# Attention and two MoE layers: weight stores of the first seven-product layer on ScalarE's queue, and its conversion steps apart

## The chip, the cores and the metric

The kernel runs on one core of a Trainium2 chip. The metric is the time of one execution on the device, in microseconds (us), as the median of several runs. In the profile, PE is TensorE (PEld its weight loads), DVE is VectorE, ACT is ScalarE, POOL is GpSimd and SP is SyncE, which here begins DMAs; SPq is SP's queue of them. L1206 is line 1206 of the kernel before.

## The reference

```python
# q, k, v: 8 batches x 8 heads x 576 tokens x 64
q_s = softmax(q, axis=-1);  k_s = softmax(k, axis=2)
attn = q_s @ (k_s^T @ v)                       # per batch and head
x = attn as 4608 tokens x 512
g = x @ w_gate                                 # 512 x 1536
x = (g * sigmoid(g) * (x @ w_val)) @ w_out     # 1536 x 512
h = x @ w_in                                   # 512 x 2048
out = where(h > 0, h, exp(min(h, 0)) - 1) @ w_out2   # 2048 x 512
```

The weights come as 64-bit floats, seen as pairs of 32-bit words.

## The kernel before

**Stages.** Tokens go in nine blocks of 512. `run_a` takes the blocks i = 0 to 8 in turn (to about 580 us): for each it works on the first half of the first MoE's features, six chunks f of 128, each in three substeps s: the gate product (`proj`), the value product, and the product with w_out of the chunk before (`emit_B`, L792 to L794). Beside this it prepares the attention of the blocks ahead: the tables `PLAN0`, `PLAN1` and `PLAN` say in which (f, s) a step such as `kv`, `turn1` or `kturn` is called, by `side_1a`. From about 580 to 1020 us the other half of the features runs with seven products in place of eight (`unit_b`, `step_b`, `single_b`, `step_s`; `product`, L1082): two blocks are cut in quarters, and the products M1 to M7 take sums of quarters of the input and of the weights. From 1020 us on the second MoE (`run_2`, `step`) does the same with its own weights.

**Splitting.** A product has 32-bit operands as a high part in a shorter format (ACT copies) and the rest (a subtraction on DVE or POOL). `part_split` (L1052 on ACT, L1053 on DVE) does this for a weight read back from DRAM; `splits` collects such jobs, `splits_due` and `run_splits` call them.

**Conversion.** `conv` is called beside the products and makes 32-bit weights of the chunks: `conv_load` (raw, SP), `conv_scale` (cg, ACT L189), `conv_bits` (DVE L204, L207, L211 into one of four buffers cd), `conv_split`. For a pair of chunks of the later half `sums_out` builds the sums of quarters on POOL (L252 to L255, st) and stores seven pieces (L265, sfg, sfv, sd); wo and wp chunks are stored by L236 (wb, wd). `defer(n, fn)` calls fn n substeps later, through `aged`.

**Attention round trips.** q is turned by way of DRAM: `qturn` (DVE, qn), `qout` (L534, dq), `qin` (L542, qT), then PE's `xT` (L622). `kturn` makes the maximum of k, stores it (L398, dk) and reads it back spread over the partitions (L400, mb). `load_q` (L353, L363) and `load_v` (L338) fetch the next block's inputs.

**Operands of the seven products.** `xd_tick` goes through six columns: it reads four quarters back (`xd_rows`, yr, L991), makes differences on POOL (`xd_open`, L1001), the high part on ACT (L1044), the low part on POOL (L1017, `xd_lo`), and stores both (L1019, xd). `x_small` and `x_big` load them for the second MoE; `load_s` and `load_p` load its weights (s<-sd, w<-wd).

Each engine takes its instructions in program order; SP is one queue, and a DMA that waits there holds all behind it.

## Time and profile before

| | |
|---|---|
| median of three runs | 1779.06 us (1778.4 to 1781.88) |
| profiled execution, its own time | 1786.1 us |
| its span | 1784.3 us |
| mean granted clock of PE | 0.974 |
| busy: PE, DVE, ACT, POOL | 1686.5, 1165.0, 799.9, 288.7 us |
| DMA | 351.95 MB, 197 GB/s over the span |

A row of waits says which instruction waited, which one released it, and for how long. A timeline row has the start, the duration, engine and line, out<-in, and the number of like instructions that were merged; the brackets give the idle time of the engine before it. In a table by stage, PEclk is the granted share of TensorE's full clock (1.00 is 2.4 GHz, 0.50 is 1.2).

### The profile page before, as it was taken

How to read it: one execution, taken by the hardware profiler on the slowest of the kernel's cores; microseconds unless marked ns; L12 is line 12 of the kernel's file. 1: busy time of each engine (PE TensorE's matmuls, PEld its weight loads, DVE VectorE, ACT ScalarE, POOL GpSimd, SP SyncE). 2: the span in 40 equal slices, each digit the busy share in tenths (PEclk: the TensorE clock that was granted, in tenths of full speed). 3: DMA queues.
4: the chain of work that ended last, by engine and by line, in shares of the span. 5: the costliest groups of instructions: out<-in, count | busy, mean ns of one | idle time of the engine just before them, and what ended most of it. 6: DMA issues, size and time to landing. Idle time of an engine off the chain costs nothing.

```text
span 1784.3 us, 22221 instructions
## 1 busy us (share of the span) xinstructions
PE 1686.5 (95%) x8228; PEld 1376.4 (77%) x8228; DVE 1165.0 (65%) x1758; ACT 799.9 (45%) x1339; POOL 288.7 (16%) x238
## 2 busy tenths in 40 slices
PE   5899898888999899998989889999999999999999
PEld 4677686666777688886878768888888888888887
DVE  7857796768667765664655476757674877466574
ACT  4635244334324442322422365646564755355353
POOL 3611132223015202353341100000000000000000
PEclk9999998998999999999999899999999999999999
DMA  9465877884667666878595945272612543352511
GB/s 279 123 166 164 245 212 226 220 257 150 220 204 284 222 235 225 291 253 313 198 355 210 395 138 222 96 271 69 250 74 100 182 189 125 135 188 72 212 48 71
DMA packets 192459, 351.95 MB, mean 197 GB/s; under 512 B 50144, under 2 KB 131040, under 8 KB 178400
## 3 DMA queue, kind: packets, MB, share of 16 engines
q1 hardware_dynamic: 192352, 350.55, 58.2%
q8 instruction: 64, 1.05, 0.2%
q14 instruction: 43, 0.35, 0.1%
HBM read 234.36 MB, written 116.14 MB: 196 GB/s over the span
## 4 chain that ended last, share of the span: by engine, by line
PE 75%; DMA 8%; DVE 7%; ACT 4%; issue 2%; POOL 2%; SPq 1%; DVEq 0%; POOLq 0%; ACTq 0%
PE p L1082 27%; PE y L794 11%; PE y L792 11%; PE y L793 11%; PE a L811 5%; PE a L812 5%; PE a L815 4%; DMA sd<-cd 1%; DMA ys<-ev 1%; DMA ev<-yp 1%; PE t L622 1%; DMA s<-sd 1%; PE t L464 1%; DVE u L1206 1%; DMA q<-in_q 1%
## 5 line engine op out<-in xcount | busy, mean ns | idle before, releaser
L1206 DVE TENSOR_TENSOR u<-u,p 128x512 f32<-128x512 f32 x315 | 216.0, 686 | 237.4 <-PE p L1082 212.8
L1082 PE MATMUL p<-xp,s 128*128 128x512 f32 x1344 | 326.0, 396 | 29.3 <-DVE u L1206 26.9
L1082 PEld LDWEIGHTS p<-xp,s 128*128 128x128 f32 x1344 | 255.0, 191 | 88.1 <-DVE u L1206 32.5
L1082 PE MATMUL p<-xs,s 128*128 128x512 f32 (+1 forms) x1260 | 274.7, 372 | 2.8 <-ACT th L1438 2.8
L1082 PEld LDWEIGHTS p<-xs,s 128*128 128x128 f32 x1260 | 224.5, 192 | 45.2 <-ACT th L1438 3.6
L794 PE MATMUL y<-w,g 128*128 128x512 f32 x576 | 225.1, 391 | 0.6
L792 PE MATMUL y<-w,g 128*128 128x512 f32 x576 | 224.3, 389 | 0.8 <-ACT g L1121 0.8
L793 PE MATMUL y<-w,g 128*128 128x512 f32 x576 | 224.2, 389 | 0.0
L811 PE MATMUL a<-x,w 128*128 128x512 f32 x424 | 174.4, 411 | 4.0 <-DVE th L842 3.0
L812 PE MATMUL a<-x,w 128*128 128x512 f32 x424 | 170.5, 402 | 0.0
L1101 DVE SCALAR_TENSOR_TENSOR th<-e,th 128x512 f32<-128x512 f32 x144 | 99.3, 690 | 101.5 <-ACT e L1096 100.0
L1094 ACT ACTIVATE e<-u 128x512 f32<-128x512 f32 x108 | 67.7, 627 | 147.5 <-DVE u L1206 147.5
L794 PEld LDWEIGHTS y<-w,g 128*128 128x128 f32 x576 | 108.1, 188 | 26.4 <-DVE g L1130 4.2
L792 PEld LDWEIGHTS y<-w,g 128*128 128x128 f32 x576 | 108.2, 188 | 23.4 <-ACT g L1121 1.2
L793 PEld LDWEIGHTS y<-w,g 128*128 128x128 f32 x576 | 108.1, 188 | 22.2
L1121 ACT ACTIVATE g<-th 128x512 fp32r<-128x512 f32 (+1 forms) x160 | 91.3, 580 | 67.8 <-DVE th L1107 67.8
L1130 DVE TENSOR_TENSOR g<-th,g 128x512 fp32r<-128x512 f32 (+1 forms) x160 | 100.0, 634 | 32.0 <-ACT g L1121 29.6
L815 PE MATMUL a<-x,w 128*128 128x512 f32 x424 | 113.8, 390 | 0.6 <-POOL w L244 0.6
L811 PEld LDWEIGHTS a<-x,w 128*128 128x128 f32 x424 | 82.9, 196 | 30.0 <-issue 7.5
L824 ACT ACTIVATE g<-th 128x512 fp32r<-128x512 f32 x54 | 33.9, 629 | 150.9 <-DVE th L842 150.9
L812 PEld LDWEIGHTS a<-x,w 128*128 128x128 f32 x424 | 83.1, 196 | 16.8
L815 PEld LDWEIGHTS a<-x,w 128*128 128x128 f32 x424 | 80.2, 189 | 18.1 <-POOL w L244 1.0
(204 smaller groups left out, 2728.3 us busy)
## 6 DMA issues: line engine op xcount, KB each, us to landing
xp<-xd SPq DMA_DIRECT2D x32, 1024.0 KB, 10.3
xs<-xd SPq DMA_DIRECT2D x51, 512.0 KB, 7.3
xd<-xst SPq DMA_DIRECT2D x42, 512.0 KB, 7.7
raw<-in_moe_w_out SPq DMA_DIRECT2D x26, 512.0 KB, 5.0
s<-sbg SPq DMA_DIRECT2D x12, 1024.0 KB, 6.9
s<-sbv SPq DMA_DIRECT2D x12, 1024.0 KB, 7.4
yp<-ev SPq DMA_DIRECT2D x9, 1024.0 KB, 4.3
xs<-ev SPq DMA_DIRECT2D x18, 512.0 KB, 6.9
```

What stands on the lines that cost most here:

```text
L792: nc.tensor.matmul(out=ps, lhsT=wh, rhs=xh, start=first, stop=False)
L793: nc.tensor.matmul(out=ps, lhsT=wh, rhs=xl, start=False, stop=False)
L794: nc.tensor.matmul(out=ps, lhsT=wl, rhs=xh, start=False, stop=last)
L811: nc.tensor.matmul(out=ps, lhsT=wh, rhs=x[:, c, 0, :], start=(c == 0), stop=False)
L812: nc.tensor.matmul(out=ps, lhsT=wh, rhs=x[:, c, 1, :], start=False, stop=False)
L815: nc.tensor.matmul(out=ps, lhsT=wl, rhs=x[:, c, 0, :], start=False, stop=(c == KD - 1))
L1082: nc.tensor.matmul(out=out_, lhsT=w, rhs=x, start=first and (q, c, k) == (0, 0, 0), stop=(c, k) == (1, 2), skip_group_check=True,)
L1094: nc.scalar.activation(out=e, in_=h, func=ACTF.Relu, scale=-1.0)
L1101: nc.vector.scalar_tensor_tensor(out=t, in0=e, scalar=1.0, in1=t, op0=ALU.add, op1=ALU.mult)
L1121: nc.scalar.activation(out=gt[:, 0, at:at + n], in_=t[:, q * n:(q + 1) * n], func=ACTF.Copy)
L1130: nc.vector.tensor_tensor(gt[:, 1, at:at + n], t[:, q * n:(q + 1) * n], gt[:, 0, at:at + n].bitcast(FP32), op=ALU.subtract,)
L1206: nc.vector.tensor_tensor(o, a, b, op=ALU.add)
```

## The change

1. The column chunks of the later weights are taken as 256 x 256 squares in another order (`wsrc_quads`, two DMAs per chunk), so that two quarters lie side by side; `sums_out` then stores four pieces, not seven. These stores, those of wb and wd, and those of yp (L868, `emit_B`) are begun on ACT's queue: 87 DMAs, where ACT had none. `conv` loads ahead of its other steps in this phase.
2. `qout` and the store of dk are called one substep later; the read of mb has a step of its own (`kspread`), `qin` of the first half and `load_q` too, and the second `qin` stands at (4, 0), not (3, 2).
3. `xd_tick`: another order of M1 to M7, with each sum made one operand ahead; rows are read up to two columns ahead and rest five ticks; the low parts go to DVE.
4. `part_split`'s subtraction can be deferred, each split can be held for some rounds, and the four first ones (`side_last`) go one per substep. `x_small` loads M7 and M5 a step earlier.

The diff, cut to its core:

```diff
@@ -79,6 +79,10 @@
...
 
+    def wsrc_quads(w, f):
+        r, c = f % 2 * 256, f // 2 * 256
+        return w[r:r + 256, c:c + 256].rearrange("(c p) (e f) -> p e c f", p=128, e=2)
+
     chunks = []
@@ -93,11 +97,11 @@
...
             for f in fs_:
-                chunks.append(((kind, f), wsrc_cols(w, f), True))
+                chunks.append(((kind, f), wsrc_quads(w, f), 2))
         for f in fs_:
...
     for f in range(F2):
-        chunks.append((("i", f), wsrc_cols(w_in2, f), True))
+        chunks.append((("i", f), wsrc_quads(w_in2, f), 2))
     for f in range(F2):
@@ -171,7 +175,11 @@
...
             rslot[n], t = slot4(kinds, [128, 512], "raw", I64)
-        if cols:
+        if cols == 2:
+            o = t.rearrange("p (e c f) -> p e c f", e=2, c=2)
+            for e in range(2):
+                nc.sync.dma_start(out=o[:, e], in_=src[:, e])
+        elif cols:
             nc.sync.dma_start(out=t.rearrange("p (c f) -> p c f", c=4), in_=src)
@@ -233,7 +241,7 @@
...
             d = ds.pop(n).bitcast(FP32)
-            defer(1, lambda: nc.sync.dma_start(out=wd[f] if kind == "p" else wb[f], in_=d))
+            defer(1, lambda: nc.scalar.dma_start(out=wd[f] if kind == "p" else wb[f], in_=d))
             return
@@ -247,8 +255,8 @@
...
         st = cv_p.tile([128, 4, 256], FP32, tag="st", name="st", bufs=1)
-        a11, a12 = d1[:, 0:256], d1[:, 256:512]
-        a21, a22 = d2[:, 0:256], d2[:, 256:512]
+        a11, a21 = d1[:, 0:256], d1[:, 256:512]
+        a12, a22 = d2[:, 0:256], d2[:, 256:512]
         nc.gpsimd.tensor_tensor(st[:, 0], a21, a22, op=ALU.add)
@@ -257,23 +265,29 @@
...
         st = sums(d1, d2)
-        srcs = [d1[:, 0:256], d1[:, 256:512], d2[:, 256:512]] + [st[:, k] for k in range(4)]
+        flat = lambda t: t.rearrange("p a n -> p (a n)")
 
         def store():
-            for a, src in enumerate(srcs):
-                part, k = PART[a]
-                nc.sync.dma_start(out=dst[part][:, k], in_=src)
+            nc.scalar.dma_start(out=dst[0][:, 0], in_=d1[:, 0:256])
+            nc.scalar.dma_start(out=flat(dst[1][:, 0:2]), in_=d2)
+            nc.scalar.dma_start(out=flat(dst[0][:, 1:4]), in_=flat(st[:, 0:3]))
+            nc.scalar.dma_start(out=dst[1][:, 2], in_=st[:, 3])
 
...
         free[0] = stage["split"]
+        ahead = stage["load"] >= NA1
+        if ahead:
+            conv_load()
+            conv_load()
         conv_split(eng or nc.gpsimd)
...
         conv_scale(wait)
-        conv_load()
-        conv_load()
+        if not ahead:
+            conv_load()
+            conv_load()
 
@@ -395,7 +409,9 @@
...
         )
-        nc.sync.dma_start(out=dk[b], in_=mk)
+        defer(0, lambda: nc.sync.dma_start(out=dk[b], in_=mk))
+
+    def kspread(b):
         mb = at1.tile([128, H, D], FP32, tag="km", name="mb")
@@ -865,7 +881,7 @@
...
                 nc.scalar.activation(out=ev[:, c, :], in_=acc[ph, i][c], func=ACTF.Copy)
-            nc.sync.dma_start(out=yps[i], in_=ev)
+            nc.scalar.dma_start(out=yps[i], in_=ev)
 
@@ -1001,12 +1017,12 @@
...
             ("M1", b11, lambda: sub(t1, b12, b11)),
-            ("M5", t1, lambda: sub(t2, b22, t1)),
-            ("M2", b21, lambda: None),
+            ("M2", b21, lambda: sub(t2, b22, t1)),
+            ("M5", t1, lambda: sub(b12, b22, b12)),
             ("M6", t2, lambda: sub(b21, b21, t2)),
+            ("M3", b22, lambda: None),
+            ("M7", b12, lambda: None),
             ("M4", b21, lambda: None),
-            ("M3", b22, lambda: sub(b12, b22, b12)),
-            ("M7", b12, lambda: None),
         ]
@@ -1014,7 +1030,7 @@
...
             m, c = xd_st["cur"][0:2]
-            nc.gpsimd.tensor_tensor(d[:, 1, :], src, d[:, 0, :].bitcast(FP32), op=ALU.subtract)
+            nc.vector.tensor_tensor(d[:, 1, :], src, d[:, 0, :].bitcast(FP32), op=ALU.subtract)
             defer(1, lambda: (
@@ -1024,11 +1040,11 @@
...
             e[0] += 1
-        if n < min(6, 2 * ready, k + 1) and room(ANY) >= 6:
+        if n < min(6, 2 * ready, k + 2) and room(ANY) >= (4 if n == k else 8):
             xd_rows(n)
...
         if xd_st["cur"] is None:
-            if k not in xd_r or xd_r[k][0] < 3:
+            if k not in xd_r or xd_r[k][0] < 5:
                 return
@@ -1040,31 +1056,37 @@
...
         at, d = slot4(ANY, [128, 2, TB], "xst")
+        nc.scalar.activation(out=d[:, 0, :], in_=src, func=ACTF.Copy)
         pre()
-        nc.scalar.activation(out=d[:, 0, :], in_=src, func=ACTF.Copy)
         xd_st["lo"] = (op, src, at, d)
...
 
-    def part_split(hi, lo):
+    def part_split(hi, lo, age=0):
         nc.scalar.activation(out=hi, in_=lo.bitcast(FP32), func=ACTF.Copy)
-        nc.vector.tensor_tensor(lo, lo.bitcast(FP32), hi.bitcast(FP32), op=ALU.subtract)
+        defer(age, lambda: nc.vector.tensor_tensor(
+            lo, lo.bitcast(FP32), hi.bitcast(FP32), op=ALU.subtract
+        ))
 
     def splits_due():
-        split_now.extend(splits)
-        splits.clear()
+        for e in list(splits):
+            if e[0]:
+                e[0] -= 1
+            else:
+                splits.remove(e)
+                split_now.append(e[1])
 
     def run_splits():
-        for fn in split_now:
-            fn()
+        for n, fn in enumerate(split_now):
+            fn(min(n // 2, 1))
         split_now.clear()
 
-    def load_p(f, kinds=ANY):
+    def load_p(f, kinds=ANY, hold=0):
         tag, t = slot4(kinds, [128, 2, 512], "w2")
         nc.sync.dma_start(out=t[:, 1].bitcast(FP32), in_=wd[f])
-        splits.append(lambda: part_split(t[:, 0], t[:, 1]))
+        splits.append([hold, lambda age: part_split(t[:, 0], t[:, 1], age)])
         W["p", f] = t
@@ -1246,6 +1268,8 @@
...
                 elu_hi(k12, e12)
+            aged()
+            aged()
             ends = [m() for m in mid]
@@ -1272,6 +1296,8 @@
...
             elu_lo(k12, e12)
+        aged()
+        aged()
         w = cg()
@@ -1309,12 +1335,14 @@
...
 
-    def load_s(g):
+    def load_s(g, hold=0):
         SW[g] = [s_tile((g + 2) % NG2, part) for part in range(2)]
...
             nc.sync.dma_start(out=t[:, :, 1, :].bitcast(FP32), in_=sd[g][part])
-            splits.append(lambda t=t: part_split(t[:, :, 0, :], t[:, :, 1, :]))
+            splits.append([
+                hold, lambda age, t=t: part_split(t[:, :, 0, :], t[:, :, 1, :], age)
+            ])
 
@@ -1391,10 +1419,10 @@
...
             nc.sync.dma_start(out=t[:, :, 1, :].bitcast(FP32), in_=sf[key][part])
-            splits.append(lambda t=t, part=part: (
-                part_split(t[:, :, 0, :], t[:, :, 1, :]),
+            splits.append([0, lambda age, t=t, part=part: (
+                part_split(t[:, :, 0, :], t[:, :, 1, :], age),
                 defer(2, lambda: nc.sync.dma_start(out=sb[key][part], in_=t.bitcast(FP32))),
-            ))
+            )])
 
@@ -1681,6 +1709,8 @@
...
                 load_yp(u[0])
+            if g == 1:
+                x_small(nxt, X_MID[0:2], ANY)
             step_s(u, g, mid, lambda: (aged(), xd_st["k"] < 6 and xd_tick(3)), g == NG1 - 1)
@@ -1690,7 +1720,7 @@
...
                 load_s(1)
-                x_small(nxt, X_MID, ANY)
+                x_small(nxt, X_MID[2:], ANY)
         while xd_st["k"] < 6 or later:
@@ -1699,9 +1729,9 @@
...
         for f in range(4):
-            load_p(f)
+            load_p(f, hold=1 + f // 2)
         carry = [lambda f=f: b_D(u[0], f) for f in (F1 - 2, F1 - 1)]
-        carry.append(lambda: (load_s(2), load_s(3), None)[2])
+        carry.append(lambda: (load_s(2), load_s(3, 1), None)[2])
         return carry
@@ -1726,7 +1756,8 @@
...
             splits_due()
-            run_splits()
+        if split_now and (ff, s) >= (3, 2):
+            split_now.pop(0)(0)
         if (ff, s) == (2, 0):
@@ -1748,7 +1779,8 @@
...
         "norm1": (2, 1), "turn1": (2, 2), "load_v2": (2, 2), "kmax0": (3, 0), "kmax1": (3, 2),
-        "xT0": (3, 2), "xT1": (3, 2), "in1": (3, 2), "kturn": (4, 0), "xT2": (5, 0), "xT3": (5, 0),
+        "in0": (2, 1), "load_q": (3, 0), "in1": (4, 0), "kspread": (4, 2),
+        "xT0": (3, 2), "xT1": (3, 2), "kturn": (4, 0), "xT2": (5, 0), "xT3": (5, 0),
         "qmax0": (4, 2), "qmax1": (5, 2),
@@ -1763,7 +1795,8 @@
...
         "qT2": (4, 0), "qT3": (4, 1), "xT2": (4, 2), "xT3": (4, 2),
-        "kmax0": (4, 1), "kmax1": (4, 2), "kturn": (5, 0), "qmax0": (5, 1), "qmax1": (5, 2),
+        "kmax0": (4, 1), "kmax1": (4, 2), "kturn": (5, 0), "kspread": (5, 2),
+        "qmax0": (5, 1), "qmax1": (5, 2),
     }
@@ -1797,8 +1830,11 @@
...
             st["sum"] = lambda: (qsum(t, 0), qsum(t, 1))
-            st["turn0"] = lambda: (qturn(t, 0), qout(t, 0), qin(t, 0))
-            st["turn1"] = lambda: (qturn(t, 1), qout(t, 1), u < NB and load_q(u))
+            st["turn0"] = lambda: (qturn(t, 0), defer(0, lambda: qout(t, 0)))
+            st["turn1"] = lambda: (qturn(t, 1), defer(0, lambda: qout(t, 1)))
+            if u < NB and i > 1:
+                st["load_q"] = lambda: load_q(u)
+            st["in0"] = lambda: qin(t, 0)
             st["in1"] = lambda: qin(t, 1)
@@ -1809,6 +1845,7 @@
...
                 st["kturn"] = lambda: kturn(u)
+                st["kspread"] = lambda: kspread(u)
         if u < NB:
@@ -1894,8 +1931,8 @@
...
                 if n == 0 and k < 2:
-                    load_p(4 + 2 * k)
-                    load_p(5 + 2 * k)
+                    load_p(4 + 2 * k, hold=1)
+                    load_p(5 + 2 * k, hold=1)
                 step(u, q, carry if k == 0 else [lambda: dd(u[0], k - 1)])
...
                 if turn:

```

On SP, in block i = 2, around the second `qin` (qT<-dq). raw, q, vtile, qT are buffers; sfv, wb, dq, dk are in DRAM. Before:

```order
L265 DMA sfv_132<-st 128x256 x3
L265 DMA sfv_133<-st 128x256
L534 DMA dq_156<-qn 32x8x128 x4
L353 DMA q<-in_q 64x2x256 x4
L363 DMA q<-in_q 64x2x256 x4
L338 DMA vtile<-in_v 128x8x64 x4
L338 DMA vtile<-in_v 64x8x64
L175 DMA raw<-in_moe_w_val 128x4x128
L177 DMA raw<-in_moe_w_out 128x512
L236 DMA wb_150<-cd 128x512
L236 DMA wb_151<-cd 128x512
L542 DMA qT<-dq_156 128x512 x2
```

and now:

```order
L558 DMA qT<-dq_156 128x512 x2
L662 DMA xs_175<-ev 128x1024
L352 DMA vtile<-in_v 128x8x64 x4
L352 DMA vtile<-in_v 64x8x64
L181 DMA raw<-in_moe_w_val 128x2x128 x2
L550 DMA dq_156<-qn 32x8x128 x4
L367 DMA q<-in_q 64x2x256 x4
L377 DMA q<-in_q 64x2x256 x4
L181 DMA raw<-in_moe_w_val 128x2x128 x2
L185 DMA raw<-in_moe_w_out 128x512
L558 DMA qT<-dq_156 128x512 x2
L412 DMA dk_163<-mk 16x32
```

The v loads stand ahead of dq, the seven sfv stores and two wb stores are gone, and dk's store and read stand right behind qT.

On ACT, in the same block, from the rest of silu (th, g) to the conversion. Before:

```order
L824 ACTIVATE g<-th 128x512
L189 ACTIVATE cg<-raw 128x512
L838 ACT_TABLE_LOAD
L838 ACTIVATE th<-a 128x512
L824 ACTIVATE g<-th 128x512
L189 ACTIVATE cg<-raw 128x512
L838 ACTIVATE th<-a 128x512
L189 ACTIVATE cg<-raw 128x512
L824 ACTIVATE g<-th 128x512
L601 ACTIVATE x<-t 128x512
```

and now:

```order
L840 ACTIVATE g<-th 128x512
L197 ACTIVATE cg<-raw 128x512
L854 ACT_TABLE_LOAD
L854 ACTIVATE th<-a 128x512
L840 ACTIVATE g<-th 128x512
L271 DMA sfv_132<-cd 128x256
L272 DMA sfv_133<-cd 128x512
L273 DMA sfv_132<-st 128x768
L274 DMA sfv_133<-st 128x256
L197 ACTIVATE cg<-raw 128x512
L854 ACTIVATE th<-a 128x512
L197 ACTIVATE cg<-raw 128x512
```

Four stores stand between two silu steps, and a wb store behind each of two conversions.

On DVE, at the passage from the first MoE's last step (silu's th and g, `step_s`) to the second MoE's first sums (u). s is a weight of the second MoE. Before:

```order
L1206 TENSOR_TENSOR u<-u,p_8250 128x512
L1053 TENSOR_TENSOR s_8175<-s_8175 128x4x256
L1053 TENSOR_TENSOR s_8176<-s_8176 128x3x256
L1053 TENSOR_TENSOR s_8179<-s_8179 128x4x256
L1053 TENSOR_TENSOR s_8180<-s_8180 128x3x256
L1547 TENSOR_TENSOR th<-th,u 128x256
L1547 TENSOR_TENSOR th<-th,p_8195 128x256
L1206 TENSOR_TENSOR u<-u,p_8250 128x512
L1206 TENSOR_TENSOR u<-u,p_8232 128x512
L1547 TENSOR_TENSOR th<-th,u 128x256 x2
L1553 TENSOR_TENSOR g_8337<-th,g_8337 128x256
L1553 TENSOR_TENSOR g_8342<-th,g_8342 128x256
```

and now:

```order
L1575 TENSOR_TENSOR th<-th,u 128x256 x2
L1581 TENSOR_TENSOR g_8319<-th,g_8319 128x256
L1581 TENSOR_TENSOR g_8324<-th,g_8324 128x256
L1581 TENSOR_TENSOR g_8319<-th,g_8319 128x256
L1581 TENSOR_TENSOR g_8324<-th,g_8324 128x256
L1069 TENSOR_TENSOR s_8169<-s_8169 128x4x256
L1069 TENSOR_TENSOR s_8170<-s_8170 128x3x256
L1069 TENSOR_TENSOR s_8173<-s_8173 128x4x256
L1069 TENSOR_TENSOR s_8174<-s_8174 128x3x256
L1228 TENSOR_TENSOR u<-u,p_8367 128x512
L1228 TENSOR_TENSOR u<-u,p_8374 128x512
L1228 TENSOR_TENSOR u<-u,p_8386 128x512
```

The four subtractions of s stood ahead of silu's last th and g; they now stand behind all of them.

## Rows read from the trace of the kernel before

**Rows 1.** Waits of PE: engine, line <- releaser: us in total, times, longest.
```profile
PE p L1082 <- DVE u L1206: 26.9, 9, 6.2
PE t L622 <- DMA qT<-dq: 20.9, 4, 6.8
PE c L622 <- DVE cd L211: 10.7, 3, 5.7
```

**Rows 2.** Table by stage: us, busy of PE, PEld, DVE, ACT, POOL; clock, DMA share, GB/s.
```profile
140.00:475.00 335.00, 303.44 (x1746) 240.05 (x1746) 252.08 (x378) 129.61 (x185) 78.69 (x76) 0.93 0.73 215
568.00:580.00 12.00, 9.01 (x33) 7.00 (x32) 9.13 (x12) 2.24 (x5) 2.19 (x2) 0.86 1.00 378
700.00:1000.00 300.00, 288.56 (x1340) 239.97 (x1339) 167.15 (x245) 96.52 (x185) 114.33 (x89) 0.98 0.76 280
1000.00:1070.00 70.00, 55.01 (x240) 44.44 (x240) 43.60 (x67) 36.22 (x60) 0.00 (x0) 0.88 0.64 234
1070.00:1784.00 714.00, 708.76 (x3272) 590.10 (x3270) 454.12 (x711) 379.66 (x657) 0.00 (x0) 1.00 0.39 144
```

**Rows 3.** The same table for the stretches at the lower granted clock.
```profile
210.10:217.00 6.90, 3.96 (x20) 2.45 (x21) 1.44 (x3) 1.49 (x3) 0.00 (x0) 0.51 0.65 245
397.90:414.90 17.00, 7.19 (x25) 4.15 (x26) 10.39 (x17) 2.75 (x5) 4.14 (x6) 0.50 0.66 210
824.50:831.40 6.90, 5.14 (x12) 4.09 (x13) 4.38 (x7) 1.64 (x3) 1.28 (x1) 0.51 1.02 359
923.50:926.90 3.40, 3.22 (x8) 2.55 (x9) 2.29 (x5) 1.64 (x3) 0.00 (x0) 0.50 0.96 282
1043.00:1049.80 6.80, 5.19 (x12) 4.13 (x13) 4.22 (x7) 4.29 (x8) 0.00 (x0) 0.50 0.74 239
```

**Rows 4.** SP's queue in order of time: start, us of issue, line, out<-in, count.
```profile
185.13 3.36 SPq L265 DMA_DIRECT2D sfv<-cd  x3
192.38 1.89 SPq L534 DMA_DIRECT2D dq<-qn  x4
199.73 4.36 SPq L338 DMA_DIRECT2D vtile<-in_v  x5
206.46 1.34 SPq L542 DMA_DIRECT2D qT<-dq  x2
985.42 12.02 SPq L1019 DMA_DIRECT2D xd<-xst  x6
```

**Rows 5.** PE in order of time; in brackets the idle time before and its releaser.
```profile
201.38 1.07 PE L815 MATMUL a<-x,w 128*128 128x512 f32 x4
206.82 1.07 PE L815 MATMUL a<-x,w 128*128 128x512 f32 x4
213.04 0.55 PE L622 MATMUL t<-qT,bd 64*64 64x192 f32 x1 [5.15 <-DMA qT<-dq]
1020.63 2.93 PE L1082 MATMUL p<-xp,s 128*128 128x512 f32 x6 [4.17 <-DVE u L1206]
1044.61 2.93 PE L1082 MATMUL p<-xp,s 128*128 128x512 f32 x6 [6.25 <-DVE u L1206]
```

**Rows 6.** DVE in order of time, the same columns.
```profile
399.69 0.69 DVE L211 SCALAR_TENSOR_TENSOR cd<-raw,c 128x512 uint32<-128x512 uint32 x1 [11.29 <-DMA sd<-cd]
564.75 7.38 DVE L1053 TENSOR_TENSOR s<-s 128x1024 fp32r<-128x1024 f32 x4
1013.68 2.10 DVE L1053 TENSOR_TENSOR s<-s 128x1024 fp32r<-128x1024 f32 x2 [10.65 <-ACT s L1052]
```

**Rows 7.** ACT in order of time, the same columns.
```profile
809.50 0.63 ACT L1044 ACTIVATE xst<-yr 128x512 fp32r<-128x512 f32 x1 [9.67 <-DMA yr<-ys]
822.04 0.63 ACT L1044 ACTIVATE xst<-yr 128x512 fp32r<-128x512 f32 x1 [2.60 <-POOL yr L1001]
1012.59 1.98 ACT L1052 ACTIVATE s<-s 128x1024 fp32r<-128x1024 f32 x2 [12.35 <-DMA s<-sd]
1029.81 3.98 ACT L1052 ACTIVATE w<-w 128x512 fp32r<-128x512 f32 x6 [5.32 <-DMA w<-wd]
```

## The prediction, made before the changed kernel ran

> **What bounds the kernel now.** I read the shares of busy time first: PE is busy almost throughout (708.76 of the last 714 us [rows 2]), so what can be won is PE's idle time and the stretches at the lower clock. The list of PE's waits says who is late [rows 1]: DVE's adds in the products (26.9 us), the read of qT back from DRAM (20.9 us), and DVE's conversion L211 (10.7 us). The table by stage says where [rows 2]: 140 to 475 us has 335.00 − 303.44 = 31.6 us of idle PE, 568 to 580 has 3.0, 700 to 1000 has 11.4, 1000 to 1070 has 15.0; after 1070 next to none, and the change moves next to nothing there. In the attention stretch neither DVE (252.08 of 335) nor the DMA engines (share 0.73) are full as a mean. The third view is the granted clock: behind a long wait PE works at 0.50, that is at 1.2 of 2.4 GHz, for 3.4 to 17 us [rows 3]. Half of the busy time in such a stretch is lost. In the attention there are four, with 3.96 busy in the first, 7.19 in the last and 20.4 in all, so 10.2 us are lost; behind the two large waits between 700 and 1000: (5.14 + 3.22) / 2 = 4.2; behind the one at 1038: 5.19 / 2 = 2.6.
>
> Why qT is late is seen on SP's queue [rows 4]. SP issues one DMA after another: the weight stores from 185.13 (the first three take 3.36 us), dq at 192.38, then eight q loads, five v loads (4.36 us), raws, two wb stores, and only at 206.46 the reads of qT that PE wants. PE ends its last L815 before them (four from 206.82) and starts on qT at 213.04, 5.15 us idle [rows 5]. The same queue holds sd stores back, so L211 waits 11.29 us for a buffer at 399.69 [rows 6].
>
> **A, the attention blocks (parts: stores to ACT, `wsrc_quads`, load_v/dq/load_q/in1 apart, kspread).** Removed from SP: 7 stores per pair, wb, wd and yps. In the block at 180 to 207 us the stores held SP from 185.13 to 192.38, 7.25 us. In the new order the v loads are ahead of dq; 185.13 + 4.36 and two raws (at 0.6 each, since two raws and two wb lie between v's end at 204.09 and 206.46) give 190.7; then dq 1.89, eight q loads (192.38 + 1.89 to v's start at 199.73, 5.4), three raws, 1.8: 199.8 for the issue of qT against 206.46 [rows 4], so 6.7 us earlier. With the same 6.6 us from issue to PE's start (206.46 to 213.04) qT is there at 206.4, and PE wants it at 213.04 − 5.15 = 207.9. The longest of the four qT waits is 6.8 us [rows 1], so 6.7 covers them all but for a tenth. L211's waits were for sd stores behind v loads; these now go from ACT as soon as their sums are there, and the raws' loads ahead of them matter no more. kspread's read stands behind its store's landing in a step of its own, so SP isn't held between the two.
> What can be won is 31.6 + 10.2 = 41.8. I take 33: the cover is between nothing and 1.5 us, and DVE has 252 of 335 us, which leaves it little to catch up with after a burst. Ends: 41.8 (all of it) and 13 (the bank waits 10.7 with one short clock stretch, 5.2 / 2, and nothing of qT, if the transfers and not the queue are slow).
>
> What this adds: ACT issues 87 DMAs, 4 per pair for 14 pairs. The trace of before has no DMA issue on ACT. By the nearest rows, SP's in this stretch, one costs 3.36 / 3 = 1.1 us, so a pair holds ACT 4.5 us; queued behind are silu's th and g, for which DVE's th and then PE's `emit_B` wait. Cover: a gate and a val product with an `emit_B` between them are 206.82 − 201.38 = 5.4 us [rows 5], and g is wanted about that much later, so 4.5 us hides. The bound above is SP in the stretch where the DMA engines are full, 12.02 us for 6 issues [rows 4], 2.0 each, 8.0 a pair; the bound below is nothing at all. I take 1.1, since it is the same stores in the same stretch.
>
> A rule of the Trainium skill speaks against this part. DMA: Bandwidth & Descriptors, section Issuing engines are not separate DMA queues, says that DMAs begun by several engines run on the same 16 DMA engines, and that this saves only the sequencer's time to begin them, usually small beside the transfer. By it the stores would be worth little here. The row is of the other size: 7.25 us of SP against 6.6 us from a read's issue to PE's start [rows 4, 5]; no run yet shows what is left on the transfer's side. By the rule A would be its lower end, 13, and the sum 20 us less; the rival "transfers" below prices that from rows alone.
>
> **B, the first splits at 560 to 572 us.** DVE runs the four s subs in one piece, 7.38 us from 564.75 [rows 6], with th of a silu behind them; PE idles 2.99 and has 0.86 of its clock over 12 us [rows 2], 1.7 lost. Now one of the four goes per substep, 1.85 us. Worth 4.7; I take 4.5 (ends 0 and 4.7). The wait at 606 us stays: DVE's order there is unchanged.
>
> **C, operands of the seven products, 700 to 1000 us.** ACT waits in order: 9.67 us at 809.50 for a row that lands late, 2.60 at 822.04 for POOL [rows 7]; silu's activations stand behind both. Rows are now fetched a column earlier and rest 5 ticks, not 3; the operand sums stand one op ahead; the 42 lo parts leave POOL, where each came between two sums. DVE takes them: 42 × 0.69 (a 128x512 pass of [rows 6]) = 29 us over 300, where DVE has 133 idle [rows 2], and nobody waits for them but stores. Worth at most 11.4 + 4.2 = 15.6. I take 12, since the first unit's row wait may only shrink; ends 15.6 and 5 (only the POOL waits).
>
> **D, the passage to the second MoE, 1000 to 1070 us.** Taken away: six w splits on ACT, 3.98 us from 1029.81 after 5.32 of waiting for their loads, ahead of the first elu [rows 7]; PE waits 6.25 us before 1044.61 for that elu [rows 5] and works at half clock behind it. They now fall in the next two steps. Added: the four s subs stand on DVE behind the rest of silu, whose activations stand on ACT behind the s hi splits, which wait 12.35 us for the s loads [rows 7]. In before the subs came at once, from 1013.68 [rows 6], and PE's products with s with them; now they come when silu's rest is through, which ACT was at 1029.81 − 5.32 = 1024.5. Four subs of 1.05 (2.10 for two) make 1028.7. From 1013.7 to 1044.6 PE had 31 us, of which it idled 4.17 and 6.25 [rows 5]: 20.5 of work, the same from 1028.7 on if no other wait is left, so 1049.2: **+5**, with the half clock behind a long wait as before. Ends: −6 (s is early enough, and only the removed 6.25 counts) and +12: M7 and M5 of the next unit, 2 MB, are now asked for ahead of s; at the 280 GB/s of this traffic [rows 2] that is 7 us more until s lands.
>
> **Nothing:** the start up to 140 us (the raws of that phase keep their layout) and everything after 1070 us, where the orders agree but for two moved pairs.
>
> **The sum.** −33 − 4.5 − 12 + 5 = −44.5. The profiled execution took 1786.1 us (span 1784.3 and 1.8 around it); 1741.6 there, and the median of the three runs, 1779.06, lies 7.0 below it: **1734.6, say 1735**.
>
> **Rivals.**
> *All of it* (chance 0.15): −41.8 − 4.7 − 15.6, D at 0: −62, 1717; 1711 with D at −6. For it: every PE wait in 140 to 475 has a releaser whose queue the change empties. Against: the margin at qT, nothing to 1.5 us.
> *Transfers, not the queue* (0.20): qT's reads take as long as they do because 16 engines are loaded (0.73 as a mean), and DVE is in bursts late with its part. A is 13: the sum −24.5, 1755. For it: 6.6 us from issue to use, long for 256 KB.
> *The queue isn't freed* (0.08): in1 is still behind eight q loads, dq and v loads, and its step is a substep later; if SP is held by a landing, qT is as late as before and A is 0: −11.5, 1767.5.
> *ACT becomes the bound* (0.09), slower: ACT is held at its stores, each behind POOL's last sum and a place in the DMA queue, with silu behind. At 2.0 us a store (the full stretch of [rows 4]) a pair holds ACT 8.0 us; 8.0 − 5.4 of cover + 2.6 of clock behind such a wait = 5.2 per pair, 14 pairs 73 us, so −44.5 + 73 = +28: 1807. It eats the whole gain at 44.5 / 14 = 3.2 a pair, which is 6.0 us per pair or 1.5 us per store; below 1.35 it costs nothing. Against: 1.1 in the same stretch.
>
> **How the numbers follow.** The forecast holds 0.48; each rival has the chance beside it. The range leaves out the slower rival and the ends of the others: 1711 (all of it, with D gaining) to 1768 (queue not freed). A measurement of this kernel can tell 0.2%, 3.6 us, from no change. Faster: 0.48 + 0.15 + 0.20 and 0.06 of the queue not freed, 0.89; the same: 0.02 of that and 0.01 of a mild ACT case; slower: the rest of ACT, 0.08.
>
> **What would show it.** A right: PE's waits for qT and for L211 under 10 us together, clock 1.00 in most blocks, qT's issue some 7 us before its use. Transfers: issue earlier, waits still there. ACT: PE or DVE waits for ACT's th in the attention, with DMA issues just ahead. B: no PE wait near 570. C: ACT's waits for rows and POOL gone. D: PE waits for s (DVE) at the passage, 10 us or more, none for w. Wrong altogether if PE's idle time from 140 to 475 us stays above 25.

## The result and the profile after

The changed kernel takes 1795.28 us (median of 4 runs, 1795.19 to 1796.45) against 1780.47 us before (4 runs, 1778.4 to 1785.69): 1.008 times the time of before, with a 95% interval of 1.0057 to 1.0104. It is slower by some 15 us; 1735, and faster, was forecast, with a range up to 1768.

PE's waits in the kernel after (what PE waits for, us in total, times, longest), to be held against [rows 1]:

```profile
PE t L638 <- DMA qT<-dq: 29.3, 4, 9.4
PE p L1104 <- DVE u L1228: 20.4, 7, 5.7
PE p L1104 <- DVE s L1069: 10.3, 1, 10.3
...
PE p L1104 <- ACT s L1068: 6.4, 1, 6.4
...
PE y L809 <- DVE w L1069: 4.2, 2, 2.3
...
PE p L1104 <- ACT u L1248: 3.1, 2, 2.8
```

L638 is L622 of before, L1104 is L1082. The waits for the conversion (10.7 us) are gone, as forecast; those for qT have grown from 20.9 to 29.3. The waits for s have grown too, on DVE from 0.5 to 10.3 and on ACT from 1.8 to 6.4, and two kinds are new: w on DVE and u on ACT. The table by stage of the kernel after, beside [rows 2] (the windows are fixed, and the kernel after is up to 8.7 us ahead of before in them; its wait of 2.7 us for th ends at 568.10 and so falls ahead of the second row):

```profile
140.00:475.00 335.00, 305.65 (x1766) 245.11 (x1767) 256.11 (x386) 135.88 (x191) 74.87 (x76) 0.95 0.70 216
568.00:580.00 12.00, 11.47 (x42) 8.81 (x43) 8.33 (x13) 8.19 (x14) 0.00 (x0) 0.86 1.00 364
700.00:1000.00 300.00, 285.57 (x1332) 239.04 (x1331) 187.64 (x284) 96.22 (x183) 55.89 (x41) 0.97 0.76 275
1000.00:1070.00 70.00, 49.74 (x212) 39.85 (x211) 36.54 (x57) 32.21 (x54) 0.00 (x0) 0.85 0.60 219
1070.00:1784.00 714.00, 706.68 (x3254) 587.96 (x3253) 455.26 (x712) 382.82 (x662) 0.00 (x0) 1.00 0.39 142
```

PE has the same 8228 matmuls in both kernels, in the same order but for a few neighbouring ones at the turns of q, so the n-th matmul of one can be set beside the n-th of the other. The difference of their start times, after minus before, tells in which stage time was won or lost:

| up to | after − before | in this stage | forecast |
|---|---|---|---|
| 93 us, the start | −1.3 | −1.3 | 0 |
| 472, the attention blocks (A) | −8.2 | −6.9 | −33 |
| 612, first splits (B) | −7.9 | +0.3 | −4.5 |
| 1012, unit operands (C) | −3.1 | +4.8 | −12 |
| 1070, the passage (D) | +2.7 | +5.8 | +5 |
| the end | +8.8 | +6.1 | 0 |

The two profiled spans differ by 8.9 us (1793.2 and 1784.3), the medians by 14.8: the profiled execution of before took 1786.1 us, 5.6 over the median above, that of the kernel after 1795.31, its median. Two kernels below (v behind qT, and the tiny loads) differ from before in the attention alone, and their traces agree with that of before to 0.7 us in each later stage. So the 5.6 us lie most likely in the attention, and A's −6.9 is, by this estimate, some −1 beside an ordinary execution of before. The same differences against the trace of before, for kernels of the next section:

| stage | A | B | C | D | the end |
|---|---|---|---|---|---|
| the changed kernel | −6.9 | +0.3 | +4.8 | +5.8 | +6.1 |
| splits at once | −4.6 | +0.5 | +6.2 | +0.8 | +2.0 |
| operand steps as before | −4.0 | −1.3 | −0.4 | +6.3 | +6.0 |
| stores on SP | −11.9 | −0.9 | +0.5 | +6.3 | +4.0 |
| three parts back | −14.0 | −1.1 | −0.7 | +0.5 | +1.6 |
| three back, v behind qT | −35.8 | −2.5 | +0.9 | +0.6 | +1.7 |
| the same, M7 and M5 behind s | −33.4 | −0.5 | +1.7 | −4.5 | +0.6 |

The first three rows have the same program in A; they differ by 2.9 us there, so a single entry is good to some 3 us.

### The profile page after: what moved, and what is told of

The parts are those of the page before. It is cut to its first block, busy times and chain, and to the rows that moved or that the text cites. A ratio compares the mean times of both kernels' runs of the same rounds, so it can differ in the third digit from the quotient of the medians.

```text
span 1793.2 us, 22155 instructions
## 1 busy us (share of the span) xinstructions
PE 1682.0 (94%) x8228; PEld 1375.0 (77%) x8228; DVE 1186.3 (66%) x1800; ACT 801.8 (45%) x1339; POOL 233.8 (13%) x196
## 4 chain that ended last, share of the span: by engine, by line
PE 73%; DMA 9%; DVE 8%; ACT 5%; issue 2%; SPq 2%; POOL 2%; ACTq 0%; DVEq 0%; POOLq 0%
PE p L1104 27%; PE y L810 11%; PE y L809 10%; PE y L808 10%; PE a L827 4%; PE a L828 4%; PE a L831 4%; DMA xd<-xst 2%; DVE u L1228 1%; DMA qT<-dq 1%; PE t L638 1%; ACT th L1117 1%; ACT e L1118 1%; DMA s<-sd 1%; PE t L480 1%
## 5 line engine op out<-in xcount | busy, mean ns | idle before, releaser
L1104 PE MATMUL p<-xp,s 128*128 128x512 f32 x1344 | 325.4, 396 | 37.2 <-DVE u L1228 20.4
L1104 PEld LDWEIGHTS p<-xp,s 128*128 128x128 f32 x1344 | 255.6, 191 | 94.8 <-DVE u L1228 24.2
L1104 PE MATMUL p<-xs,s 128*128 128x512 f32 (+1 forms) x1260 | 274.4, 372 | 3.1 <-ACT u L1248 3.1
L1104 PEld LDWEIGHTS p<-xs,s 128*128 128x128 f32 x1260 | 224.1, 191 | 45.0 <-ACT u L1248 3.7
L827 PE MATMUL a<-x,w 128*128 128x512 f32 x424 | 171.1, 403 | 4.5 <-DVE th L858 2.7
L828 PE MATMUL a<-x,w 128*128 128x512 f32 x424 | 167.6, 395 | 0.0
L808 PEld LDWEIGHTS y<-w,g 128*128 128x128 f32 x576 | 108.9, 189 | 24.8 <-ACT g L1143 1.7
L831 PE MATMUL a<-x,w 128*128 128x512 f32 x424 | 114.4, 392 | 0.6 <-POOL w L252 0.6
L827 PEld LDWEIGHTS a<-x,w 128*128 128x128 f32 x424 | 81.1, 191 | 29.9 <-issue 7.5
L831 PEld LDWEIGHTS a<-x,w 128*128 128x128 f32 x424 | 80.1, 189 | 17.9 <-POOL w L252 1.1
L828 PEld LDWEIGHTS a<-x,w 128*128 128x128 f32 x424 | 81.2, 191 | 16.3
L1117 ACT ACTIVATE th<-e 128x512 f32<-128x512 f32 x144 | 91.1, 633 | 4.6
```

Source lines behind the costliest of these rows:

```text
L808: nc.tensor.matmul(out=ps, lhsT=wh, rhs=xh, start=first, stop=False)
L827: nc.tensor.matmul(out=ps, lhsT=wh, rhs=x[:, c, 0, :], start=(c == 0), stop=False)
L828: nc.tensor.matmul(out=ps, lhsT=wh, rhs=x[:, c, 1, :], start=False, stop=False)
L831: nc.tensor.matmul(out=ps, lhsT=wl, rhs=x[:, c, 0, :], start=False, stop=(c == KD - 1))
L1104: nc.tensor.matmul(out=out_, lhsT=w, rhs=x, start=first and (q, c, k) == (0, 0, 0), stop=(c, k) == (1, 2), skip_group_check=True,)
L1117: nc.scalar.activation(out=t, in_=e, func=ACTF.Tanh, scale=-0.5)
```

## The experiments

All times are medians. Each kernel was timed on one chip together with the kernel before, in five groups, in which before took 1780.2 to 1782.7 us; the changed kernel's 1795.28 was timed beside 1780.47. So a difference of 2 or 3 us between two groups is not safe by itself.

**Splits at once.** In the changed kernel:

```diff
-        defer(age, lambda: nc.vector.tensor_tensor(
-            lo, lo.bitcast(FP32), hi.bitcast(FP32), op=ALU.subtract
-        ))
+        nc.vector.tensor_tensor(lo, lo.bitcast(FP32), hi.bitcast(FP32), op=ALU.subtract)
```

> The changed kernel, but part_split's subtraction on DVE is done at once again (holds, loads and all else as changed). Theory P (the deferred subtractions cost): PE's 10.3 us wait for s at 1026 us goes or falls under 3, the 2.8 us wait at 1411 and the half clock behind it go (6 us there), the w waits at 1054 and 1073 (2.3 and 1.9) go; some 2 us may come back near 566. 1795 - 12 = 1783, between 1778 and 1788. Rival Q (the stores on ACT slow everything): no change beyond 2 us, 1795.

Measured 1784.75: 10.5 us less than the changed kernel. Deferring the subtractions costs 10.5 us, at two places. At the passage, DVE in the kernel after:

```profile
1024.18 1.42 DVE L1581 TENSOR_TENSOR g<-th,g 128x256 fp32r<-128x256 f32 x4
1025.52 4.09 DVE L1069 TENSOR_TENSOR s<-s 128x1024 fp32r<-128x1024 f32 x4
```

Silu's last g ends first, then come the four subtractions, and PE waits 10.3 us for them. Without the deferral that wait is gone; the wait for s on ACT stays (6.6 us), and so do those for w (4.6 us), which I had expected to go. The second place is at 1390 us, where I had put nothing. DVE there, in the kernel before and then in the kernel after:

```profile
1384.95 0.69 DVE L1107 TENSOR_TENSOR th<-th,u 128x512 f32<-128x512 f32 x1
1385.56 4.09 DVE L1053 TENSOR_TENSOR s<-s 128x1024 fp32r<-128x1024 f32 x4
1389.57 0.76 DVE L1130 TENSOR_TENSOR g<-th,g 128x256 fp32r<-128x256 f32 x2
```

```profile
1388.22 0.69 DVE L1129 TENSOR_TENSOR th<-th,u 128x512 f32<-128x512 f32 x1
1393.16 0.76 DVE L1152 TENSOR_TENSOR g<-th,g 128x256 fp32r<-128x256 f32 x2 [4.25 <-ACT g L1143]
1393.84 4.09 DVE L1069 TENSOR_TENSOR s<-s 128x1024 fp32r<-128x1024 f32 x4
```

Before, the four subtractions filled the time in which DVE had to wait for ACT's g anyway. One pair further on, DVE first idles 4.25 us and then does them, with every later step of elu behind: PE waits 2.8 us at 1411 and runs at the lower clock after it (0.62 granted as a mean from 1411.5 to 1416).

**Operand steps as before.** In the changed kernel, the order of M1 to M7, the sums, the low parts on POOL, the fetching of rows, and the ticks are taken from the kernel before.

> The changed kernel, but the operand steps of the seven products (order of M1 to M7, sums, low parts, row fetch) as before. Theory P (operand buffers wait for their stores, 4.7 to 5.1 us each): the 3.8 us wait at 724, and one or two us at 816 and 915, go: 1795 - 4.5 = 1790.5, between 1787 and 1793; ACT's waits for xd stores vanish and those for rows and POOL are back. Rival Q (the part is worth its 12 us and hides a loss elsewhere): slower, 1800 or more.

Measured 1792.13, 3.2 less. ACT in the changed kernel, behind four operands in a row:

```profile
711.11 0.62 ACT L1059 ACTIVATE xst<-yr 128x512 fp32r<-128x512 f32 x1
715.43 0.63 ACT L1473 ACTIVATE g<-th 128x512 fp32r<-128x512 f32 x1 [3.70 <-DVE th L1469]
716.75 0.63 ACT L1473 ACTIVATE g<-th 128x512 fp32r<-128x512 f32 x1 [0.69 <-DMA xd<-xst]
722.45 1.15 ACT L1059 ACTIVATE xst<-yr 128x512 fp32r<-128x512 f32 x2 [5.07 <-DMA xd<-xst]
```

ACT's waits from 700 to 1000 us, two of the kernel before and then one of the kernel after:

```profile
ACT xst L1044 <- POOL yr L1001: 22.9, 9, 3.5
ACT xst L1044 <- DMA yr<-ys: 20.7, 3, 9.7
```

```profile
ACT xst L1059 <- DMA xd<-xst: 13.5, 3, 5.1
```

The waits for POOL and for late rows (which fall to 8.5) give way to a wait for a free buffer: an operand buffer comes free only when its store has landed. Three such waits take 13.5 us, in the same place ahead of silu's g. By the times alone the 3.2 us are not clear of noise (1.0034 to 1.0073 times before, against 1.0057 to 1.0104); the stages place the gain: C goes from +4.8 to −0.4, and A, where the program is the same, takes 2.9 of it back.

**Stores on SP.** In the changed kernel, the 87 stores are begun by `nc.sync` again, still four per pair.

> The changed kernel, but the weight stores (four per pair, wb, wd) and yp are begun on SP again, at the same places in the program. Theory P (SP and ACT hold each other: SP's q loads wait for a store that ACT has not begun yet, and both queues' issues get slower): the relief and the harm cancel, the qT waits (29.3 us) stay within 5, the time within 4 us of 1795. Rival Q (stores on ACT are the harm): qT waits fall by 10 or more, 1783 or less. Rival R (stores on ACT are a gain that something else eats): qT waits grow by 10 or more, 1805 or more.

Measured 1784.20, 11.1 less, with 19.0 us of qT waits. My theory P (neither gain nor harm) fell: the stores on ACT are harm (rival Q, whose 1783 is missed by 1.2 us). In the two profiles 5.0 us of it lie in A and 4.3 in C; but C varies by itself, from 0.0 to +6.2 in the kernels that have these operand steps and the stores on ACT. SP in block i = 3 of the changed kernel, and then with the stores on SP (start, us of issue):

```profile
246.97 7.90 SPq L352 DMA_DIRECT2D vtile<-in_v  x5
...
256.14 2.13 SPq L550 DMA_DIRECT2D dq<-qn  x4
259.58 6.28 SPq L367 DMA_DIRECT2D q<-in_q  x4
265.90 2.49 SPq L377 DMA_DIRECT2D q<-in_q  x4
...
269.43 1.02 SPq L558 DMA_DIRECT2D qT<-dq  x2
```

```profile
250.71 7.04 SPq L352 DMA_DIRECT2D vtile<-in_v  x5
...
259.03 2.02 SPq L550 DMA_DIRECT2D dq<-qn  x4
261.09 2.42 SPq L367 DMA_DIRECT2D q<-in_q  x4
263.56 1.86 SPq L377 DMA_DIRECT2D q<-in_q  x4
```

Begun by ACT, the stores left the v loads a start 3.7 us earlier; but the first four q loads took 6.28 us, not 2.42. Why is in the list of what SP waited for from 140 to 475 us in the changed kernel (two waits of the q loads for stores, one of the v loads), and on ACT in the same block:

```profile
SPq L367 <- DMA sd<-cd: 7.9, 3, 3.7
...
SPq L367 <- DMA sfg<-cd: 4.4, 1, 4.4
...
SPq L352 <- DMA xs<-ev: 2.8, 1, 2.8
```

```profile
263.78 0.63 ACT L840 ACTIVATE g<-th 128x512 fp32r<-128x512 f32 x1 [2.95 <-DVE th L858]
263.79 0.33 ACTq L271 DMA_DIRECT2D sfg<-cd  x1
```

A load of q waits for the landing of a store of weights with which it shares nothing but a place in the count of DMAs under way: in the trace the DMAs of SP and ACT report their landing by the same eight semaphores, and a DMA waits for the one before it on its semaphore. The fourth q load and the first sfg store have the same one. The store is on ACT's queue behind silu's g and begins at 263.79; the q load begins at 265.54, and SP stood still for an instruction of ACT. In the blocks i = 2 to 5 together the eight q loads took 30.4 us of SP, against 18.3 with the stores on SP, and the v loads 29.1 against 25.1.

**v behind qT.** In the kernel before, in `PLAN`:

```diff
-        "norm1": (2, 1), "turn1": (2, 2), "load_v2": (2, 2), "kmax0": (3, 0), "kmax1": (3, 2),
-        "xT0": (3, 2), "xT1": (3, 2), "in1": (3, 2), "kturn": (4, 0), "xT2": (5, 0), "xT3": (5, 0),
+        "norm1": (2, 1), "turn1": (2, 2), "kmax0": (3, 0), "kmax1": (3, 2),
+        "xT0": (3, 2), "xT1": (3, 2), "in1": (3, 2), "load_v2": (4, 1), "kturn": (4, 0), "xT2": (5, 0), "xT3": (5, 0),
```

> The kernel before, with one step moved: the v loads of the next block (five DMAs) at (4, 1), behind the second read of qT, not at (2, 2) ahead of it. Theory P (the length of SP's queue ahead of qT is what PE waits for): qT is asked for 4 to 5.5 us earlier, its waits fall from 20.9 to under 6 us, half clock behind two of them goes: 1779 - 16 = 1763, between 1758 and 1769. Rival Q (the transfers themselves are the limit): qT lands as late, 1779 within 4.

Measured 1759.32, 0.9871 times before (0.9843 to 0.9898). qT waits 2.1 us in all:

```profile
PE t L622 <- DMA qT<-dq: 2.1, 1, 2.1
```

One line takes away the qT waits that part A of the change was to take away; the conversion's stay (9.0 us).

**Three parts back**, and **the stores on ACT alone.** The first undoes the three parts above together; the second adds to the kernel before only the squares and the stores on ACT.

> The changed kernel with three parts undone together: subtractions of part_split at once, operand steps as before, and weight and yp stores on SP (four per pair). What is left of the change is the four stores in place of seven, the moved attention steps, the holds and the earlier x_small. Theory P (the three losses lie in different stages and add: 10.5, 3 and 11): 1795 - 24.5 = 1770.5, between 1767 and 1775. Rival Q (they overlap, a stage that is relieved meets the next wait): 1779 or more.

> The kernel before with one part of the change alone: columns taken as squares, four stores per pair, and these, wb, wd and yp begun on ACT; the order of dq, q, v and qT is as before. Theory P (SP waits for places in the DMA queue that a store not yet begun by ACT holds, and two queues slow each other): no gain from the emptier queue, qT waits stay at 15 to 30 us, the waits for L211 fall under 4; 1776 to 1786. Rival Q (an emptier SP queue brings qT earlier, as the prediction had it): qT and L211 waits both under 8, 1755 or less.

Measured 1772.72 and 1780.79 (1.0007 times before, 0.9993 to 1.002). The three losses add nearly (10.5 + 3.2 + 11.1 = 24.8; 22.6 measured); what is left of the change (four stores in place of seven, the loads ahead in `conv`, the moved attention steps, the first splits apart, the splits held back, `x_small` earlier) is faster than before by 0.43%. The squares and the stores on ACT alone are worth nothing: 29.6 us of qT waits take the place of the conversion's.

**The stores on POOL**, and **later in the program.** In the changed kernel, `nc.gpsimd` in place of `nc.scalar`; or `defer(3, store)` in place of `defer(2, store)`.

> The changed kernel with the same stores begun on POOL's queue in place of ACT's; POOL's DMAs count on semaphores of their own. Theory P (SP's q loads are held by the places they share with ACT's stores): SP isn't held any more, qT waits fall from 29.3 by 8 or more, 1783 to 1787, unless POOL itself is held, which shows as waits of DVE for st or cd. Rival Q (the load on the transfers, or two queues at once, makes it slow): qT waits within 5 of 29.3, 1793 to 1797.

> The changed kernel with the four stores of a pair called three substeps later instead of two, still on ACT: they then stand behind the eight q loads in the program, and no q load shares a place with a store that ACT hasn't begun. Theory P (the holds are what the ACT stores cost): the q loads take 4 to 5.5 us in every block, not 8 to 9 in three of them, qT waits fall from 29.3 by 9 or more, 1795 - 12 = 1783, between 1779 and 1787. Rival Q (two queues at once are slow, or the transfers): qT waits within 5 of 29.3, 1791 or more.

Measured 1792.37 and 1790.64: both only 3 to 5 us less, short of what theory P asked. On POOL's queue no q load waits for a store any more, but the v loads still take up to 9.1 us and qT waits 25.3 us. Called later, the stores stand behind the q loads of block i = 3, which then take 2.40 and 1.86 us, and the wait for qT there is 4.0, not 8.3; in the next two blocks other stores took the places, and the waits are 6.8 and 8.4. So SP's waits behind ACT are shown where they could be taken away, and they are not all of the 11 us: the v loads are as slow with the stores on POOL's queue. What slows them stays open.

**v behind qT in the changed kernel**, with and without the parts undone:

> The changed kernel with one step moved: the v loads at (4, 1), behind the second read of qT. Theory P (length of the queue ahead of qT; 6 to 9 us of issue go away): qT waits fall from 29.3 to under 10, with most of the half clock behind them, 1795 - 24 = 1771, between 1766 and 1778. Rival Q (SP then stands at its places behind ACT's stores as long as before): qT waits over 18, 1785 or more.

> The kernel with three parts undone (subtractions at once, operand steps as before, stores on SP, four per pair) and the v loads at (4, 1). Theory P (PE waits for what stands ahead of qT on SP): the 17.4 us of qT waits and most half clock behind them go, 1772.7 - 21 = 1752, between 1747 and 1757. Rival Q (what is moved behind qT meets the next use: v late, or the stores behind it stall DVE's L219): L219 or v waits over 8 us take its place, 1762 or more.

> As the one with three parts undone and v later, but the stores are on ACT (two parts undone). Theory P (ACT's stores cost only as far as they hold what stands ahead of qT, and with v behind it there is room): within 5 of its twin, 1752 to 1758. Rival Q (they cost by themselves, by slow issue or ACT's own time): 8 us or more slower than the twin.

Measured 1769.01 (26 less than the changed kernel), 1751.70 with three parts back, and 1758.42 with two, that is with the stores on ACT. The stores on ACT cost 6.7 us even with v out of the way, more than theory P allowed; one qT wait of 6.2 us comes back, in a block whose eight q loads take 6.4 us against 4.1.

**M7 and M5 behind s.** As the one with three parts back and v later, with `x_small(nxt, X_MID, ANY)` again behind `load_s(1)`.

> As the one with three parts undone and v later, and the loads of M7 and M5 of the next unit again behind the loads of s. Theory P (2 MB ahead of s make PE wait 6.3 us for s at the passage): that wait falls to 2, 4 to 7 us faster than its twin. Rival Q (s is late for another reason): within 2 of it.

Measured 1748.33, 3.4 less than its twin (4 to 7 were expected), 0.9805 times before (0.9789 to 0.9822), the fastest kernel here. PE's first wait at the passage, without and with this edit:

```profile
979.93 3.33 PE L1102 MATMUL p<-xp,s 128*128 128x512 f32 x6 [6.36 <-ACT s L1068]
```

```profile
980.97 0.73 PE L1102 MATMUL p<-xp,s 128*128 128x512 f32 x2 [1.33 <-ACT s L1068]
```

**SP's time or the bytes?** v behind qT takes both away. First the v loads went to POOL's queue, in the kernel before; then, with v behind qT, twelve loads of 1 KB that nobody reads were put in v's old place.

> The kernel before, but the v loads of the blocks from i = 2 on are begun on POOL's queue, at the same step (in two halves each, ten DMAs of 256-byte runs): SP no longer spends its 4.4 to 5.7 us on them, and the same bytes still start ahead of qT. Theory S (SP's time to begin DMAs is what makes qT late): qT is asked for 4 to 5 us earlier and its waits fall from 20.9 to under 10; 1768 or less. Theory T (what must pass through the same transfer engines ahead of qT makes it late, whoever begins it): qT is asked for earlier or not, but the waits stay over 15; 1775 or more.

> The kernel before with the v loads behind qT (as the one at 1759 us), and in their old place, ahead of qT, twelve tiny DMAs of 1 KB each that nobody reads: SP's time to begin them (12 at 0.35 us or more) is back, the 1.1 MB of v are not. Theory S (SP's time makes qT late): qT waits are back at 15 us or more, 1773 or more. Theory T (the bytes ahead of qT on full transfer engines make it late): qT waits stay under 6, 1764 or less.

The first took 1796.31, with 22.5 us of qT waits. By the letter that is theory T, but POOL began the ten loads 3 to 7 us apart and held up its own sums behind them, and the conversion once made PE wait 15.5 us, so the time decides nothing. By blocks it leans to S: in i = 2 SP asked for qT at 200.76, not 206.46, and in i = 2 to 4 PE waited 2.6, 3.5 and 0.2 us for it, not 5.2, 6.8 and 2.4; 16.1 us of the 22.5 are one wait in i = 5. The second took 1786.84, 27.5 us more than without the twelve, and the qT waits are back. PE's waits, and SP in block i = 2:

```profile
PE t L628 <- DMA qT<-dq: 22.5, 4, 9.3
```

```profile
194.11 2.57 SPq L359 DMA_DIRECT2D q<-in_q  x4
196.72 2.62 SPq L369 DMA_DIRECT2D q<-in_q  x4
199.39 5.68 SPq L346 DMA_DIRECT2D tiny<-in_v  x12
...
207.17 1.15 SPq L548 DMA_DIRECT2D qT<-dq  x2
```

The 12 KB are a hundredth of what v's loads move (1.1 MB), so it is SP's time at the DMAs ahead of qT that PE waits for: 5.68 us here, up to 6.62 in the other blocks, of 24.5 us in all 3.8 spent on waiting for places of the q loads. The share of the DMA engines confirms it. Ahead of qT in block i = 3, with v behind qT and then with the twelve loads (us, busy of PE, PEld, DVE, ACT, POOL; clock, DMA share, GB/s):

```profile
244.00:263.00 19.00, 19.00 (x96) 15.11 (x95) 18.14 (x32) 5.22 (x9) 3.64 (x4) 1.00 0.98 305
```

```profile
251.00:273.00 22.00, 18.40 (x92) 14.32 (x90) 18.00 (x31) 5.82 (x10) 3.65 (x4) 1.00 0.78 240
```

With the DMA engines full (0.98) PE has no idle time and finds qT there; with engines less loaded (0.78) it waits for qT. The reads of qT from 140 to 475 us land as fast in all three kernels: a median of 3.1 us from issue to landing before, 3.0 with v behind qT, 3.0 with the twelve loads. So the rival "transfers, not the queue" falls.

## Why the prediction was wrong, step by step

- **What bounds the attention** was right: SP's queue ahead of qT, shown by v behind qT (−21) and by the twelve tiny loads (+27.5).
- **A failed at "185.13 + 4.36 ... 199.8 for the issue of qT".** It took the v and q loads at the durations that they had in another place of the queue. Seven stores did leave SP (they had held it for 6.3 of the 7.25 us; the rest SP stood still), but in block i = 2 the v loads took 8.81 us in place of 4.36, and in i = 3 the q loads 8.8 in place of 4.8; qT was asked for at 204.22 (not 199.8), 269.43 (before: 269.79), 333.65 (329.85) and 400.35 (398.88). PE's idle time from 140 to 475 us is 29.35 us, above the 25 that the prediction named as "wrong altogether". The rival "the queue isn't freed" named the mechanism, SP held by a landing, with a chance of 0.08; it should have had most of it, though its 1767.5 was 28 us too low as well, for B, C and the end.
- **The stores** cost 11 us on ACT, where I had looked for a cost on ACT alone (1.1 us a store, hidden); some 5 of them lie in A, by SP's waits and slower loads (5.3 where the stores on ACT are tried with v behind qT), and the rest is not placed safely. The rival in which ACT is the bound didn't happen: no wait of PE for ACT's silu is among the new ones. That the result is slower, as this rival had it, is no point for it. Its 2.0 us a store was misread: the six issues in 12.02 us take 0.32 us each, and SP stood between them.
- **The rule of the Trainium skill** (DMA: Bandwidth & Descriptors, section Issuing engines are not separate DMA queues) that I set aside would have forecast the stores' worth better: alone they were worth nothing (1.0007). That section of the Trainium skill calls the time to begin a DMA usually small beside the transfer. Here the runs differ: with the tiny loads it made 27.5 us. The stores were worth nothing alone because what they took away (10.7 us of waits for the conversion) came back at qT (from 20.9 to 29.6).
- **B**: DVE's piece of four is cut up. DVE in the kernel after, around the step th that PE waits for:

```profile
563.07 2.31 DVE L1069 TENSOR_TENSOR s<-s 128x1024 fp32r<-128x1024 f32 x1
565.30 1.28 DVE L1404 TENSOR_TENSOR xs<-v,xs 128x512 fp32r<-128x512 f32 x2
566.50 0.95 DVE L1069 TENSOR_TENSOR s<-s 128x768 fp32r<-128x768 f32 x1
567.37 0.68 DVE L858 TENSOR_TENSOR th<-th,a 128x512 f32<-128x512 f32 x1
```

  The pieces (2.31 and 0.95 us) still stand ahead of th, with operand steps between; PE's wait for th is 2.7 us in place of 3.0, and the stage gave nothing (+0.3 for −4.5). No run took these pieces apart further.
- **C failed at "nobody waits for them but stores".** The low parts and the stores behind them set when a buffer comes free, and ACT waits for that: 13.5 us in three waits, +4.8 in place of −12. The wait takes the gain in every kernel with these steps (12.4 to 14.6 us of it in five others); how much is lost on top varies: C is between 0.0 and +6.2 in the six of them, and between −1.7 and +1.7 in the five with the steps undone. Which of the steps makes the wait (the order, the rows held longer, the low parts on DVE) no run separates.
- **D was right in size, in part by luck**: +5.8 against +5. The subtractions behind silu cost 10.3 us of waiting, and without the deferral the stage is at +0.8; that is the step that the sum had. M7 and M5 ahead of s, left to the end of the range, cost as much (PE's wait 5.0 us longer, +0.6 against −4.5 in the stage, 3.4 us of time), and what the held-back splits of w won (PE's wait of 6.25 us there is 0.81 now) made up for it. That no wait for w would be left was wrong: 4.2 us.
- **"Nothing after 1070" was wrong by 6.1 us.** Two moved pairs were seen in the order and taken for nothing, because no wait of before stood there. The four subtractions had just filled a gap; what counts of a moved instruction is what its new place pushes, not whether its old place was waited for.

In the profiles 53.3 us lie between the forecast (−44.5) and the result (+8.8): 26.1 of them are A's, 16.8 C's, 6.1 the end's and 4.8 B's; D's 0.8 and the start (−1.3) are the rest.

## What to carry to other kernels

When a queue is the bound, move what is not wanted soon behind what is wanted now; giving it to another engine's queue was worth nothing here (1.0007), in part since it left the count of DMAs under way as it was and let one engine's queue stand still for the other's compute. Price a moved DMA by the time that it takes in its new place, waits for landings included, and price a deferred instruction by what it pushes. Full DMA engines are not yet a bound: whether a wait goes when the queue ahead of it gets shorter has to be tried.

## What was not expected of the hardware

The DMA engines were full just ahead of each qT wait (a share of 0.94 to 1.12), which the mean over the stage (0.73) hid, and still they were not what PE waited for. The kernel before, table of stretches:

```profile
190.00:213.00 23.00, 17.89 (x90) 13.89 (x88) 17.23 (x29) 5.82 (x10) 2.88 (x4) 0.94 1.00 276
251.00:276.00 25.00, 18.39 (x92) 14.31 (x90) 17.97 (x31) 5.81 (x10) 3.64 (x4) 0.91 1.00 281
```

Twelve loads of 1 KB took 0.47 us each of SP's queue (5.68 us in all, short waits between them included), not much less than loads of q of 128 KB (0.64, 2.57 us for four). The five v loads, which move the same bytes every time, held SP from 4.36 to 8.81 us. Of the 8.81 the five issues take 4.81 and the waits between them the rest, 2.8 of it for the landing of a load of xs; in the 7.90 us of the next block one issue alone takes 3.49. Why an issue gets that slow no run shows.
